# FFT filter and squared-ReLU FFN in one kernel: the FFT units of a batch spread over its whole period

## The chip, the cores and the metric

The kernel runs on one core of a Trainium2 chip. The metric is device time in microseconds. TensorE does the matmuls, VectorE (DVE) and ScalarE (ACT) empty PSUM and do elementwise work, GpSimd (POOL) and SyncE (SP) here mostly issue DMAs, each in its own order. The engines run side by side and wait for each other at semaphores.

## What is computed

```python
def _attn_ref(x, filt_r, filt_i):            # x: 8 x 3008 x 256
    X = np.fft.rfft(x, axis=1)
    F = (filt_r + 1j * filt_i)[None, :, :]
    Y = X * F
    return np.fft.irfft(Y, n=x.shape[1], axis=1).astype(np.float32)

def _moe_ref(x, w_in, w_out):                # x: 24064 x 256, w_in: 256 x 2048
    h = np.maximum(x @ w_in, 0.0)
    return (h * h @ w_out).astype(np.float32)
```

Each of the 8 batches is filtered along its 3008 positions; the result, as 24064 tokens, goes through two layers with a squared ReLU between them.

## The kernel before

**The FFT of a batch** is done by matmuls with constant matrices (3008 = 64 x 47), in four kinds of units:

- A (`unit_a`, L345): 16 a batch; one matmul of 512 columns into a psF tile, copied to `u` by ACT (even units, L362) or DVE (odd, L364); each four units are written to DRAM (`dU`) by SP. `load_x` (L186, POOL's queue) brings its input, two loads to a tile of four units.
- `read_u` (L429) brings a batch's `dU` back in another layout into the single buffer `ut`.
- B (`unit_b`, L436): 12 a batch; two matmuls of 256 columns into psF; DVE multiplies by the filter into `prod` (L450), and POOL issues two DMAs that add the halves of `prod` (L457).
- P (`unit_p`, L480): 12 a batch; two matmuls into psF, copied by ACT to `ze` (L489); each three units are written to DRAM (`dZ`, L492).
- `read_z` (L501) brings a quarter of `dZ` back into a tile `zt` by two DMAs (halves of the frequencies). The second half of every quarter needs the last P unit.
- Y (`unit_y`, L509): 16 a batch; four matmuls of 94 columns into psF, copied to `yt` by ACT (even) or DVE (odd, L532). Units 4c to 4c+3 read quarter c and give a quarter of the batch's tokens.

All psF tiles share two PSUM buffers, so a unit can only start when the unit two before it has been copied out.

**The FFN** goes over 47 groups of 512 tokens, each in 8 slots. In a slot, `ffn_g1` (L537) does four matmuls of 512 columns (more, where a group crosses a batch) and ACT's ReLU into `h`; `ffn_sq` (L559) squares on DVE, two slots at a time. The second layer of a group runs in the eight slots after, in one of two ways. The plain one (`ffn_g2`, L566) takes 64 matmuls of 256 columns. The other (`sums`, L627, and `products`, L655) takes seven products of half-size blocks instead of eight, 112 matmuls of 128 columns, for four sums on DVE and three adds into the output (L681, L687); the weights' own sums are made once (`make_t`, L611). `SEVEN` (L795) says which groups take it: from 9 on, save the last.

**The order** is written out by hand: every engine's instructions stand in program order. `fft_plan(b)` (L690) puts each unit of a batch at a slot relative to the batch's first one and at one of two places in it: 0, after the first layer's matmuls, or 1, after the second layer's. A batch's period is 48 slots (40 for batch 1). Batch b + 1's A units end where its `read_u` starts, five slots before its B. Batch 0 and most of batch 1's A units run in a prologue. The first tokens of batch b are needed by the first layer 48 slots after the batch's first (40 for batch 1).

```python
for s in range((NG + 1) * SLOTS):
    g, k = divmod(s, SLOTS)
    if g < NG:
        ffn_g1(g, k)
    run(work, s, 0)
...
    if (s - 1) // SLOTS - 1 in SEVEN:
        products((s - 1) // SLOTS - 1, (s - 1) % SLOTS)
    if g > 0 and g - 1 not in SEVEN:
        ffn_g2(g - 1, k)
    run(work, s, 1)
```

## Time and profile before

| | us |
|---|---|
| median of 3 runs | 782.75 (781.9 to 782.78) |
| the profiled execution | 782.47 |
| its span, first to last instruction | 780.7 |
| TensorE matmuls busy | 755.4 |
| DVE busy | 627.2 |
| ACT busy | 561.6 |
| POOL busy | 193.0 |

The granted TensorE clock is full throughout. Busy times of different engines overlap; a stretch's length is set by the engine that waits least in it. DVE's costs in the steady part, each from its group: a square of two slots 1218 ns (L564), a sum about 1217 ns (L639 to L648), an add into the output about 417 ns (L681, L687), a `prod` 1219 ns (L450), an A copy 683 ns (L364), a Y copy 546 ns (L532). ACT's: a ReLU 1024 ns (L557), a `ze` copy 588 ns (L489), an A copy 573 ns (L362), a Y copy 468 ns (L530).

### The profile page before, as it was taken

Reading aid. Unit: us, or ns where it says so; the run is one execution under the profiler, and the core shown is the slowest. Engines: PE = TensorE matmul, PEld = TensorE weight load, DVE = VectorE, ACT = ScalarE, POOL = GpSimd, SP = SyncE. Lnnn points to the kernel's source line nnn. Section 1 sums busy time; section 2 is a strip of 40 time slices with the busy share of each in tenths; the row PEclk is TensorE's granted clock in tenths of the full one; section 3 lists DMA queues with packets and bytes.
Section 4 is the critical chain, followed back from the end, with each engine's and each line's share of the span. In section 5 each row is a group of like instructions: output and inputs, shape, how many; then the busy total and the mean of one; then the engine's idle time right before and its main releaser. Section 6 shows DMA issues by size and latency. Waiting matters only on the chain. (4 is left out here: it accounts for less than half of the span.)

```text
span 780.7 us, 18857 instructions
## 1 busy us (share of the span) xinstructions
PE 755.4 (97%) x7878; PEld 552.5 (71%) x7878; DVE 627.2 (80%) x699; ACT 561.6 (72%) x785; POOL 193.0 (25%) x260
## 2 busy tenths in 40 slices
PE   8989999999999999999999999999999999999998
PEld 6746667667676676876778767777767767777776
DVE  6856644567778997899978999899988999987874
ACT  3976776767777677776777777776777767777774
POOL 3801730036100561005500065002840035100000
PEclk9999999999999999999999999999999999999999
DMA  9985974369534795167953578525875355521011
GB/s 365 375 253 160 149 161 116 89 158 175 136 80 119 169 171 145 57 180 130 171 116 96 173 127 149 154 76 158 149 145 126 89 151 128 128 78 55 29 55 55
DMA packets 104941, 109.20 MB, mean 140 GB/s; under 512 B 9640, under 2 KB 93096, under 8 KB 102936
## 3 DMA queue, kind: packets, MB, share of 16 engines
q1 hardware_dynamic: 85704, 87.38, 37.3%
q0 software_dynamic: 19008, 20.43, 19.5%
q8 instruction: 62, 1.02, 0.6%
q10 hardware_dynamic: 144, 0.18, 0.1%
q14 instruction: 23, 0.19, 0.1%
HBM read 58.12 MB, written 48.23 MB: 136 GB/s over the span
## 5 line engine op out<-in xcount | busy, mean ns | idle before, releaser
L557 ACT ACTIVATE h<-psH 128x1024 f16<-128x1024 f32 x376 | 384.6, 1024 | 172.2 <-PE psH L553 170.3
L553 PE MATMUL psH<-yt,sWin 128*128 128x512 f16 (+7 forms) x1728 | 386.9, 351 | 1.5 <-DVE yt L532 0.5
L564 DVE TENSOR_TENSOR h<-h 128x2048 f16<-128x2048 f16 (+1 forms) x192 | 229.6, 1196 | 64.8 <-ACT h L557 64.3
L457 POOL DMA_DIRECT2D prod<-prod x168 | 141.1, 997 | 463.7 <-DVE prod L450 458.4
L553 PEld LDWEIGHTS <-sWin 128*128 128x128 f16 x1728 | 153.4, 98 | 98.5 <-issue 3.4
L666 PEld LDWEIGHTS <-sum 128*128 128x128 f16 x2368 | 146.8, 98 | 27.2 <-issue 6.1
L666 PEld LDWEIGHTS <-h 128*128 128x128 f16 x1776 | 110.3, 98 | 22.5
L450 DVE TENSOR_TENSOR prod<-psB,sF 128x1024 f16<-128x1024 f32 x84 | 102.4, 1219 | 14.4 <-PE psB L442 14.4
L666 PE MATMUL psX<-sT,sum 128*128 128x128 f16 x1184 | 84.2, 219 | 0.0
L573 PE MATMUL psO<-sWout,h 128*128 128x256 f16 x640 | 81.8, 272 | 0.0
L573 PEld LDWEIGHTS <-h 128*128 128x128 f16 x640 | 62.0, 98 | 14.6 <-issue 0.2
L532 DVE CAST yt<-psY 128x376 f16<-128x376 f32 x62 | 33.8, 546 | 34.4 <-PE psY L523 34.4
L489 ACT CAST ze<-psP 128x512 f16<-128x512 f32 x84 | 49.4, 588 | 13.4 <-PE psP L487 8.9
L666 PE MATMUL psY<-sT,sum 128*128 128x128 f16 x592 | 57.2, 219 | 0.0
L666 PE MATMUL psY<-sWout,sum 128*128 128x128 f16 x592 | 44.9, 219 | 5.5 <-DVE bot L681 5.5
L364 DVE CAST u<-psA 96x512 f16<-96x512 f32 x50 | 34.1, 683 | 17.1 <-PE psA L358 14.9
L523 PE MATMUL psY<-sC,zt 112*128 112x94 f16 x512 | 42.4, 205 | 5.1 <-DMA zt<-dZ 4.9
L195 POOL DMA_DIRECT2D x<-in_x_dram x40 | 46.1, 1151 | 0.0
L642 DVE TENSOR_TENSOR sum<-sum,h 128x2048 f16<-128x2048 f16 x37 | 45.2, 1221 | 0.9
L666 PE MATMUL psY<-sWout,h 128*128 128x128 f16 x592 | 45.2, 219 | 0.0
L666 PE MATMUL psX<-sT,h 128*128 128x128 f16 x592 | 45.1, 219 | 0.0
L639 DVE TENSOR_TENSOR sum<-h 128x2048 f16<-128x2048 f16 x37 | 44.9, 1215 | 0.1
(88 smaller groups left out, 706.0 us busy)
## 6 DMA issues: line engine op xcount, KB each, us to landing
zt<-dZ SPq DMA_DIRECT2D x64, 192.0 KB
dU<-u SPq DMA_DIRECT2D x28, 384.0 KB
prod<-prod POOLq DMA_DIRECT2D x168, 64.0 KB, 3.6
dZ<-ze SPq DMA_DIRECT2D x28, 384.0 KB
x<-in_x_dram POOLq DMA_DIRECT2D x40, 192.0 KB, 5.3
ut<-dU SPq DMA_DIRECT2D x7, 1024.0 KB
xw<-in_x_dram SPq DMA_DIRECT2D x6, 1024.0 KB
ut<-dU SPq DMA_DIRECT2D x7, 512.0 KB
```

The costliest lines, as they stand in the source:

```text
L195: nc.gpsimd.dma_start(out=t, in_=v[:, m, :])
L450: nc.vector.tensor_mul(out=prod, in0=ps.rearrange("p (a d) -> p a d", d=D).unsqueeze(1).to_broadcast([128, 2, 2, D]), in1=sF[:, :, 2 * p:2 ...
L457: nc.gpsimd.dma_start(out=prod[64 * i:64 * i + 64, 0], in_=prod[64 - 64 * i:128 - 64 * i, 1], accum_op=mybir.AluOpType.add)
L489: nc.scalar.copy(out=zes[(b, c)][:, 2 * i6:2 * i6 + 2, :], in_=ps.rearrange("p (a d) -> p a d", d=D))
L523: nc.tensor.matmul(ps[:, 94 * jj:94 * jj + 94], zt[:, 4 * (g % 2) + jj, dt * 128:(dt + 1) * 128], sSY, start=True, stop=True)
L553: nc.tensor.matmul(ps[:, i, o:o + n], sWin[:, dt, jt * 128:(jt + 1) * 128], yts[b][:, dt, r:r + n], start=(dt == 0), stop=(dt == 1))
L557: nc.scalar.activation(out=h2[:, 2 * s:2 * s + 2, :], in_=ps, func=AF.Relu)
L564: nc.vector.tensor_mul(out=v, in0=v, in1=v)
L573: nc.tensor.matmul(pso[g][:, t % 2, :], h2s[g][:, jt, t * 128:(t + 1) * 128], sWout[:, jt, :], start=(jt == 0), stop=(jt == NJT - 1))
L639: nc.vector.tensor_add(out=t, in0=a21, in1=a22)
L642: nc.vector.tensor_sub(out=t, in0=f[5], in1=a11)
L666: nc.tensor.matmul(o[:, t, :], f[p][:, q, 128 * t:128 * t + 128], sg["w"][p][:, q, :], start=(m == 0 and p in (1, 2)), stop=(q == 7), skip ...
```

## The change

The plan now works in half slots, and units of one batch are spread over its period:

- A of batch b (3 and later) runs from slot -56 to -14.5 of the batch, one unit every 2.75 slots, a period ahead of its own B; all its copies go to ACT. A of batch 2 runs one unit every 1.25 slots from -30, with copies as before. `load_x` moves with A. Before the loads of batch 2, POOL copies one element of the current slot's `h` (`hold`), so that a load isn't issued before that slot.
- B runs from -5 to 38 instead of 18 to 36, and P 5 slots after its B, so from 0 to 43 instead of 22.5 to 40.5. Batch 1 keeps its B slots, with P 4.5 slots later. `prod` has five buffers instead of four.
- `read_z` of the four quarters stands at 43, 43.5, 48 and 54 instead of 41.5 (three) and 47.5; there are two `zt` tiles instead of three. The Y units stand at `YN`, from 45 to 72, instead of two a slot from 45 to 52.5. For batch 1 all of this is 7 slots earlier.
- `SEVEN` starts at group 6 instead of 9, and `make_t` does one of its four sums in each of four slots.

```diff
-    p_prod = ctx.enter_context(tc.tile_pool(name="p_prod", bufs=4))
+    p_prod = ctx.enter_context(tc.tile_pool(name="p_prod", bufs=5))
...
+    def hold(g, s):
+
+        nc.gpsimd.tensor_copy(out=tiny, in_=h2s[g][0:1, 2 * s, 0:1])
...
-        if a % 2 == 0:
+        if a % 2 == 0 or b > 2:
             nc.scalar.copy(out=o, in_=pv)
...
-    ztiles = [const.tile([112, 8, D], F16, name=f"zt_{c}") for c in range(3)]
+    ztiles = [const.tile([112, 8, D], F16, name=f"zt_{c}") for c in range(2)]
...
-        zt = ztiles[c % 3]
+        zt = ztiles[c % 2]
...
-        def put(r, place, f, *a):
-            plan.setdefault((r, place), []).append((f, a))
-
+        def put(r, f, *a):
+            r = int(2 * r)
+            plan.setdefault(divmod(r, 2), []).append((f, a))
+
+        d = 0
         if b == 1:
             for n in range(4, 16):
-                put(n if n < 8 else n + 2 if n < 12 else 2 * n - 7, n % 2, unit_y, 0, n)
+                put(YN[n] - (45, 45, 46, 46)[n // 4], unit_y, 0, n)
+            put(8, read_z, 0, 3)
             for k in range(4):
-                put((4, 5, 7, 7)[k], 1, cast_wout, k, nc.vector)
-        t0 = 2 if b == 1 else 5
-        for a in range(12 if b == 1 else 0, 16):
-            put(t0 + a // 2, a % 2, unit_a, b, a)
-        put(10 if b == 1 else 13, 1, read_u, b)
-        t0 = 14 if b == 1 else 18
+                put((4.5, 5.5, 7.5, 7.5)[k], cast_wout, k, nc.vector)
+            for a in range(12, 16):
+                put(2 + a / 2, unit_a, b, a)
+            put(10.5, read_u, b)
+            d = 7
+        elif b == 2:
+            for a in range(16):
+                if a % 2 == 0:
+                    put(-37 + 1.25 * a, hold, 0, 0)
+                    put(-37 + 1.25 * a, load_x, b, a // 2)
+                put(-30 + 1.25 * a, unit_a, b, a)
+            put(-8.5, read_u, b)
+        else:
+            for a in range(16):
+                if a % 2 == 0:
+                    put(-66 + 2.75 * a, load_x, b, a // 2)
+                put(-56 + 2.75 * a, unit_a, b, a)
+            put(-9, read_u, b)
         for p in range(12):
-            r = t0 + (15 if b == 1 else 18) * p // 11
-            put(r, 0, unit_b, b, p)
-            if b + 1 < B and 2 <= p < 10:
-                put(r, 0, load_x, b + 1, p - 2)
-            put(r + 4, 1, unit_p, b, p)
-        t0 = 34 if b == 1 else 41
+            r = 14 + 15 * p / 11 if b == 1 else -5 + 43 * p / 11
+            put(r, unit_b, b, p)
+            put(r + (4.5 if b == 1 else 5), unit_p, b, p)
         for c in range(4):
-            put(t0 if c < 3 else t0 + 6, 1, read_z, b, c)
+            put((43, 43.5, 48, 54)[c] - d, read_z, b, c)
         for n in range(16):
-            put((38 if b == 1 else 45) + n // 2, n % 2, unit_y, b, n)
+            put(YN[n] - d, unit_y, b, n)
         return plan
+
+    YN = (45, 45.5, 46, 46.5, 47.5, 49, 50.5, 52, 54, 56, 58, 60, 63, 66, 69, 72)
...
-    for c in range(2, 4):
-        read_z(0, c)
-
-    SEVEN = range(9, NG - 1)
+    read_z(0, 2)
+
+    SEVEN = range(6, NG - 1)
...
         for (r, place), w in fft_plan(b).items():
-            work.setdefault((first + r, place), []).extend(w)
+            for f, a in w:
+                if f is hold:
+                    a = divmod(first + r, SLOTS)
+                work.setdefault((first + r, place), []).append((f, a))
...
-        if s == SEVEN[0] * SLOTS:
-            make_t()
+        if SEVEN[0] * SLOTS <= s < SEVEN[0] * SLOTS + 4:
+            make_t(s % SLOTS)
```

More of the change, by code (lines that the diff above doesn't have):

```diff
@@ L257 @@
     sSP = const.tile([128, NC, 128], F16, name="sSP")
+    tiny = const.tile([1, 1], F16, name="tiny")
     sign = const.tile([128, 1], F32, name="sign")
@@ L609, with make_t @@
     sg = {}
-    def make_t():
-        t = p_t.tile([128, 4, 8, 128], F16, tag="t", name="sT")
+    def make_t(k):
         w = sWout.rearrange("p (q e) c -> p q e c", e=2)
@@ L616, in make_t @@
         b21, b22 = w[:, :, 1, 0:128], w[:, :, 1, 128:256]
-        nc.vector.tensor_sub(out=t[:, 0], in0=b12, in1=b11)
-        nc.vector.tensor_sub(out=t[:, 1], in0=b22, in1=t[:, 0])
-        nc.vector.tensor_sub(out=t[:, 2], in0=b22, in1=b12)
-        nc.vector.tensor_sub(out=t[:, 3], in0=b21, in1=t[:, 1])
+        if k == 0:
+            sg["t"] = p_t.tile([128, 4, 8, 128], F16, tag="t", name="sT")
+        t = sg["t"]
+        i0, i1 = ((b12, b11), (b22, t[:, 0]), (b22, b12), (b21, t[:, 1]))[k]
+        nc.vector.tensor_sub(out=t[:, k], in0=i0, in1=i1)
         sg["w"] = {1: b11, 2: b21, 3: b22, 4: t[:, 3], 5: t[:, 0], 6: t[:, 1], 7: t[:, 2]}
```

## The prediction

> **What bounds the kernel now.** I read the windows view first, with one stretch per batch: from the first matmul that a batch's Y units issue to the same matmul of the next batch. Columns: us, then busy time (and instructions) of PE, PEld, DVE, ACT, POOL, then granted clock, DMA share and GB/s.

> ```profile
> core 0: us, PE busy (x) PEld busy (x) DVE busy (x) ACT busy (x) POOL busy (x), PEclk, DMA share, GB/s
> ...
> 309.40:403.10 93.70, 91.17 (x1024) 68.11 (x1025) 84.13 (x94) 68.83 (x101) 24.07 (x32) 1.00 0.61 136
> 403.10:496.30 93.20, 91.17 (x1024) 68.56 (x1025) 84.10 (x94) 68.73 (x101) 24.07 (x32) 1.00 0.62 137
> ```

> A batch takes 93.7 us. Its matmuls need less. In the trace, matmuls of 512, 256 and 128 columns follow each other every 216, 109 and 56 ns. The 48 slots of a batch hold 192 first-layer matmuls of 512 columns (48 x 4 x 0.216 = 41.5 us), six groups of 112 products (37.5), and the FFT: A 16 x 0.216, B and P 24 x 0.109 each, Y 64 x 0.042 (11.4 in all). That makes 90.4 us, so TensorE is the bound and about 3.2 us per batch are gaps. DVE is at 84 of 93.7: close, so bursts can make TensorE wait. Which gaps they are is in the waits of PE:

> ```profile
> PE psY L666 <- DVE bot L681: 5.5, 5, 1.2
> PE psY L523 <- DMA zt<-dZ: 4.9, 7, 1.4
> ...
> PE psP L487 <- DMA prod<-prod: 2.6, 4, 0.7
> ...
> PE psP L487 <- DVE prod L450: 0.5, 2, 0.3
> ```

> The view counts idle time. Each gap costs some 0.16 us more, because a matmul is shown longer (379 ns) than the distance at which the next follows (216). Adding that, the DVE waits and the late prod transfers cost some 12 us over the whole run (with the small ones on psB and psX), and the waits for zt in batches 2 to 7 cost 4.5. The last are the end of a round trip through DRAM: the last product (unit P 11), its copy to ze, the write to dZ, the read into zt, the first Y unit. The timeline shows it for batch 3 (the row at 306.35 is SP's in a narrower window, where the reads that wait stand alone), and below it the start of batch 2's:

> ```profile
> 300.61 0.38 PE L487 MATMUL psP<-prod,sSP 128*128 128x256 f16 x2
> 301.06 0.58 ACT L489 CAST ze<-psP 128x512 f16<-128x512 f32 x1
> 302.38 0.40 SPq L604 DMA_DIRECT2D out_dram<-top  x1
> 302.87 0.45 SPq L492 DMA_DIRECT2D dZ<-ze  x1
> 306.35 2.19 SPq L505 DMA_DIRECT2D zt<-dZ  x5
> 309.44 0.33 PE L523 MATMUL psY<-sC,zt 112*128 112x94 f16 x4 [0.90 <-DMA zt<-dZ]
> ```

> ```profile
> 206.69 0.38 PE L487 MATMUL psP<-prod,sSP 128*128 128x256 f16 x2
> 206.89 1.02 ACT L557 ACTIVATE h<-psH 128x1024 f16<-128x1024 f32 x1 [0.23 <-PE psH L553]
> 207.81 0.58 ACT L489 CAST ze<-psP 128x512 f16<-128x512 f32 x1
> ```

> See three links in batch 3: from the product to the end of the copy 1.03 us; write issued 302.87, the read that needs it issued 306.35, so 3.48 us; then 3.09 us until the Y matmul runs. The write also stood behind an output store on SP's queue (301.64 to 302.87). Product to Y took 8.83 us here; in the seven batches it takes 8.0 to 8.8. In batch 2 the product follows straight on a first-layer matmul, so its copy waits for that ReLU and ends 1.70 us after the product.

> [...]

> **The change part by part.**

> *Seven products from group 6.* Groups 6, 7 and 8 go from 64 matmuls of 256 columns (64 x 0.1092 = 6.99 us) to 112 of 128 (6.25): -0.74 each, **-2.2 us**. DVE gets four sums (1.22 each) and three adds (0.42) more per group, 11.0 us in all with the squares; beside two to three prod and one or two Y copies that stays under the 15 us of a group. make_t in four slots (0.69 each) is hidden in DVE's slack.

> *Spreading.* DVE's load in the worst group before was 11.0 + 5 x 1.22 = 17 us, over the group's 15; after, prod come every 3.9 slots (2 or 3 a group) and for batches over 2 the eight A copies (0.68) are ACT's (0.57 each: ACT goes from 69 to 73 of 94). No group is then over 15. The bot waits and the late prod transfers go: **-12 us** (bounds -9 and -14; if DVE's spare were used up by something else they stay, +12 on my sum). x loads on POOL and read_u, 5 slots ahead of its B as before, keep their lead: 0.

> *The end of a batch.* P 11 moves from slot 40 (second half) to 43 (first half), read_z from 41 to 43, and Y 0 stays at 45. What was 4.5 slots is now 2. Between P 11 and Y 0 stand on PE: P 11, B 0 of the next batch and A 1 of the next but one (0.22 each) and two slots of 14 products and 4 first-layer matmuls (1.64 each, as 210.31 to 211.95 in the trace): 3.94 us. The round trip: copy end 1.70 (P now follows straight on first-layer matmuls, as in batch 2), write to read 3.2 (mean of seven, 3.0 to 3.5), read to Y 3.2 (3.0 to 3.6); SP has no store ahead in slot 43, which saves the 0.7 to 1.2 of before. 8.2 us; bounds 7.6 and 9.0. PE stands for 4.3 us before Y 0, with everything queued behind it. A 1 waits first: psF has two buffers, P 11 has its buffer until the copy ends, so 1.2 us of the 4.3 fall there. Six batches, with less PE work beside the last two (no A, no B): 4 x 4.3 + 4.5 + 4.7 = 26.4, less the 4.5 that were paid: **+21.9 us** (bounds 18 and 27).

> *Batch 1.* Same 4.5 slots, but read_z goes from slot 34.5 to 36, behind the store of slot 35. At 206.68 such a store held SP 2.2 us, until 3.1 us after the second layer's last matmuls began to drain. So the read is issued 3.6 us after slot 36 starts and lands near 6.7, while PE arrives at 4.6: **+2.1** (0 to 3). Y 3 of batch 1 now has B 1 of batch 2 ahead of it on DVE, and the first-layer matmuls behind it need it: **+0.7** (0 to 1.2).

> *psF.* A unit waits until the unit two before it is copied: some 1.6 us after an ACT unit in a slot's first half, 1.7 after a prod. The trace has that wait exactly: B 4 of batch 1 at 82.78, its prod until 84.42, P at 84.47 held for 0.44 us (0.27 idle and the 0.16).

> ```profile
> 82.78 0.38 PE L442 MATMUL psB<-ut,sSB 128*128 128x256 f16 x2
> 83.20 1.22 DVE L450 TENSOR_TENSOR prod<-psB,sF 128x1024 f16<-128x1024 f32 x1 [0.88 <-PE psB L442]
> 84.47 0.38 PE L487 MATMUL psP<-prod,sSP 128*128 128x256 f16 x2 [0.27 <-DVE prod L450]
> ```

> Laid over the new plan, slots 8 to 44 (A of batch 2 put among B, P and Y of batches 0 and 1) have 14 such pairs, 13 short by 0.3 to 0.6 us and one by 1.2: 6 us, against 1.6 before: **+4.5** (1 to 7). From batch 2 on, A 2 after Y 0 and B 3 after Y 8 are short by 0.3 and 0.5: **+3.5** over the run (0 to 6).

> *hold and the two z buffers.* Eight tiny POOL copies in slots 3 to 20 read h, so DVE's square waits for POOL there, behind up to two prod issues (1 us each). The groups there use the plain second layer and DVE has over 5 us spare a group: 0, at worst +1. A z buffer's last Y unit runs 1.5 slots or more before its next read, and the later quarters of Y end 8 slots or more before the first layer takes them: 0. Prod's fifth buffer and one memset (0.9 us) less: 0; gains are excluded, as nothing waits on them now.

> **Sum** on the profiled execution (span 780.7, its own time 782.47, so 1.8 around it): 780.7 - 2.2 - 12 + 21.9 + 2.1 + 0.7 + 4.5 + 3.5 = 799.2, hence 801.0. The median of the runs is 0.3 above that execution, less than the sum can tell.

> **Rivals.**
> *Faster.* The round trip is short in quiet queues. Then only the removals count: 780.7 - 2.2 - 12 - 4.5 + 3 = 765, time 767. For it: the reads before were issued six at once and stood behind stores. Against: the write alone took over 3.0 us in all seven batches, and batch 1, without a store ahead of it, still needed 3.1 for it. It decides at 8.2 - 18.5 / 6 = 5.1 us product to Y; below that the change wins.
> *The clock falls.* [...] Against: A 1 splits the wait in batches 2 to 5, leaving 3 us; only 6 and 7 have it whole.
> *DVE waits stay.* Prod after Y copies and squares still crowd the first slots of a group, and the 12 us are paid as well: 813. Against: nine us more slack a batch, and each stand of PE lets DVE catch up.

> **How the numbers follow.** Forecast 0.80, faster 0.07, no change (trip of about 5.1 us) 0.03, clock 0.06, DVE 0.04. The forecast's own bounds are 790 to 810; the range 787 to 812 leaves out most of the first rival, and half of the last two. 0.2% is 1.6 us, about what this kernel's runs can tell from no change. Faster 0.07, same 0.03, slower 0.90.

> **What would show it.** Right: PE waits for zt<-dZ of some 3 us in each of six batches; waits on bot and on prod transfers nearly gone; batch stretches of 95 to 96 us with PE busy the same; psA waiting on ze in slot 43. Wrong: P 11 to Y 0 under 5.5 us, or a batch stretch under 93, or PEclk under 1.00.

## The result, and the profile after

| | before | after |
|---|---|---|
| median, us | 782.33 | 830.8 (829.91 to 831.84) |
| span of the profiled execution, us | 780.7 | 829.6 |
| ratio | 1 | 1.062 (1.0602 to 1.0639) |

The change makes the kernel 6.2% slower, 48.5 us. The prediction said slower, but 801, and at most 812.

The windows view of the changed kernel, cut at the first Y matmul of batches 2, 3 and 4 (us, busy time of PE, PEld, DVE, ACT, POOL, clock, DMA share, GB/s), and the stretch from batch 2 to 3 before (the one from 3 to 4 stands in the prediction, at 309.40):

```profile
243.50:342.40 98.90, 92.77 (x1026) 68.34 (x1026) 80.13 (x86) 73.15 (x108) 24.08 (x32) 0.98 0.56 129
342.40:440.90 98.50, 92.87 (x1025) 68.92 (x1026) 80.22 (x86) 73.26 (x108) 24.09 (x32) 0.98 0.57 129
```

```profile
215.50:309.40 93.90, 91.15 (x1024) 67.17 (x1024) 84.12 (x94) 69.13 (x101) 24.07 (x32) 1.00 0.60 135
```

These two stretches take 98.9 and 98.5 us instead of 93.9 and 93.7. DVE's busy time fell from 84 to 80 us and ACT's rose from 69 to 73, as meant; both are far under the length of the stretch. The clock is no longer 1.00. In PE's waits the line for zt is now 32.4 us, where it was 4.9 before, and the waits for `bot` are gone:

```profile
PE psY L528 <- DMA zt<-dZ: 32.4, 10, 4.5
PE psA L363 <- ACT ze L494: 5.1, 7, 1.2
...
PE psB L447 <- ACT yt L535: 2.2, 6, 0.4
PE psA L363 <- DVE yt L537: 1.8, 2, 1.0
...
PE psP L492 <- DMA prod<-prod: 1.3, 2, 0.6
```

The timeline at the end of batch 3, the same place as shown of before. The SP row at 337.33 is from a narrower window, where the reads that waited for the write stand alone:

```profile
332.40 0.38 PE L492 MATMUL psP<-prod,sSP 128*128 128x256 f16 x2
332.62 0.38 PE L447 MATMUL psB<-ut,sSB 128*128 128x256 f16 x2
333.52 0.58 ACT L494 CAST ze<-psP 128x512 f16<-128x512 f32 x1
334.12 0.38 SPq L497 DMA_DIRECT2D dZ<-ze  x1
334.15 0.38 PE L363 MATMUL psA<-x,sC 94*96 94x512 f16 x1 [1.15 <-ACT ze L494]
336.03 1.01 POOL L199 DMA_DIRECT2D x<-in_x_dram  x1
337.33 1.28 SPq L510 DMA_DIRECT2D zt<-dZ  x3
342.36 0.33 PE L528 MATMUL psY<-sC,zt 112*128 112x94 f16 x4 [4.54 <-DMA zt<-dZ]
```

P 11 runs at 332.40, Y 0 at 342.36: 9.96 us, with 3.9 us of TensorE's own work between them. First A waits 1.15 us for the psF buffer that P 11's copy frees, then Y 0 waits 4.54 us for the read. Of the three links of the trip, the copy ends 1.70 us after the product and the read that needs the write goes out 3.21 us after it, both as forecast; the read until Y 0 takes 5.03 us instead of 3.2. Just after, TensorE runs at half speed. The windows view over that stretch:

```profile
342.36:342.94 0.58, 0.58 (x12) 0.58 (x13) 0.00 (x0) 0.22 (x1) 0.00 (x0) 1.00 0.10 21
342.94:346.36 3.42, 3.42 (x23) 2.17 (x21) 1.68 (x2) 1.21 (x3) 0.00 (x0) 0.50 0.02 5
346.36:350.00 3.64, 3.64 (x49) 2.95 (x48) 2.49 (x5) 2.88 (x5) 0.00 (x0) 1.00 0.00 0
```

The eighth column is the clock: 0.50 for 3.42 us, in which 23 matmuls run where the next 3.64 us hold 49. There are eight such stretches, one for batch 0 and one for each later batch, of 3.4 or 6.8 us, 41.0 us in all.

To see where the 48.9 us of span went, I took from each execution the distance from each matmul's start to the next one's, less the distance that its columns need at full clock, and put what is left down to the matmul that came late or to the half clock (us; under "prologue" everything up to 48 us but the warm-up; a row is good to somewhat under a microsecond):

| | before | after |
|---|---|---|
| needed by the columns | 744.6 | 742.4 |
| half clock, warm-up at the start | 1.5 | 2.5 |
| half clock, later | 0.2 | 17.7 |
| Y matmuls of batch 0 | 0 | 5.6 |
| Y matmuls of batch 1 | 0.4 | 3.3 |
| Y matmuls of batches 2 to 7 | 4.5 | 25.8 |
| A matmuls (psF) | 0.3 | 10.2 |
| second-layer products waiting for DVE | 6.9 | 0 |
| P matmuls | 5.0 | 3.0 |
| B matmuls | 0.8 | 3.2 |
| first layer, psO, prologue | 9.3 | 8.5 |

The seven products and DVE's relief are there, 2.2 and 6.9 us. They are outweighed fivefold by the waits of Y units (30 us more, nearly all of it for zt) and by the clock (18).

### The profile page after: what moved, and what is told of

Its sections match the earlier page's. It is cut to its first block, busy times and chain, and to the rows that moved or that the text cites. A ratio compares the mean times of both kernels' runs of the same rounds, so it can differ in the third digit from the quotient of the medians.

```text
span 829.6 us, 19171 instructions
## 1 busy us (share of the span) xinstructions
PE 773.1 (93%) x8022; PEld 562.8 (68%) x8022; DVE 622.7 (75%) x679; ACT 581.9 (70%) x831; POOL 194.0 (23%) x268
## 3 DMA queue, kind: packets, MB, share of 16 engines
q8 instruction: 63, 1.03, 0.5%
## 4 chain that ended last, share of the span: by engine, by line
PE 83%; DMA 8%; ACT 4%; DVE 3%; issue 1%; SPq 0%; POOL 0%; ACTq 0%; DVEq 0%; POOLq 0%
PE psH L558 36%; PE psX L671 17%; PE psY L671 12%; DMA zt<-dZ 5%; PE psO L578 4%; DMA dZ<-ze 3%; PE psY L528 3%; PE psA L363 2%; PE psB L447 2%; ACT h L562 2%; PE psP L492 2%; PE warm L277 1%; DVE prod L455 1%; ACT ze L494 1%; PE psf L296 1%
## 5 line engine op out<-in xcount | busy, mean ns | idle before, releaser
L558 PE MATMUL psH<-yt,sWin 128*128 128x512 f16 (+7 forms) x1728 | 392.7, 355 | 2.0 <-DVE yt L537 1.2
L671 PEld LDWEIGHTS <-sum 128*128 128x128 f16 x2560 | 161.8, 99 | 26.0 <-issue 3.6
L671 PEld LDWEIGHTS <-h 128*128 128x128 f16 x1920 | 120.0, 98 | 15.9
L671 PE MATMUL psX<-sT,sum 128*128 128x128 f16 x1280 | 95.0, 224 | 0.0
L528 PE MATMUL psY<-sC,zt 112*128 112x94 f16 x512 | 45.1, 214 | 33.9 <-DMA zt<-dZ 32.4
L528 PEld LDWEIGHTS <-zt 112*128 112x128 f16 x512 | 36.2, 103 | 57.1 <-issue 39.8
L671 PE MATMUL psY<-sT,sum 128*128 128x128 f16 x640 | 62.3, 220 | 0.0
L578 PE MATMUL psO<-sWout,h 128*128 128x256 f16 x448 | 59.2, 279 | 0.0
L367 ACT CAST u<-psA 96x512 f16<-96x512 f32 x90 | 52.3, 581 | 7.0 <-PE psA L363 5.5
L578 PEld LDWEIGHTS <-h 128*128 128x128 f16 x448 | 44.2, 100 | 14.6 <-issue 4.2
L535 ACT CAST yt<-psY 128x376 f16<-128x376 f32 x66 | 31.1, 472 | 27.6 <-PE psY L528 26.4
L647 DVE TENSOR_TENSOR sum<-sum,h 128x2048 f16<-128x2048 f16 x40 | 48.9, 1223 | 1.1
L653 DVE TENSOR_TENSOR sum<-h,sum 128x2048 f16<-128x2048 f16 x40 | 48.7, 1218 | 0.0
```

What stands on the lines that cost most here:

```text
L367: nc.scalar.copy(out=o, in_=pv)
L528: nc.tensor.matmul(ps[:, 94 * jj:94 * jj + 94], zt[:, 4 * (g % 2) + jj, dt * 128:(dt + 1) * 128], sSY, start=True, stop=True)
L558: nc.tensor.matmul(ps[:, i, o:o + n], sWin[:, dt, jt * 128:(jt + 1) * 128], yts[b][:, dt, r:r + n], start=(dt == 0), stop=(dt == 1))
L578: nc.tensor.matmul(pso[g][:, t % 2, :], h2s[g][:, jt, t * 128:(t + 1) * 128], sWout[:, jt, :], start=(jt == 0), stop=(jt == NJT - 1))
L647: nc.vector.tensor_sub(out=t, in0=f[5], in1=a11)
L653: nc.vector.tensor_sub(out=t, in0=a12, in1=f[6])
```

## The experiments

The theory: P 11 to Y 0 is a round trip through DRAM of about 8 us or more (8.1 to 8.8 before and 7.8 to 10.0 after, in batches 2 to 7), the change gives it two slots, and the stand that follows (a pause in which TensorE waits) also sets the clock to half. Rivals: spreading the units is the cost and Y only shows it; the clock falls for another reason; what lies beside the trip (x loads, read_u) makes it long.

**The round trip alone, in the kernel before (e7_late).**

```diff
-            put(r + 4, 1, unit_p, b, p)
+            if b == 1 or p < 11:
+                put(r + 4, 1, unit_p, b, p)
+            else:
+                put(43, 0, unit_p, b, p)
...
-            put(t0 if c < 3 else t0 + 6, 1, read_z, b, c)
+            put(*((t0, 1) if b == 1 and c < 3 else (43, 0) if c < 3 else (t0 + 6, 1)), read_z, b, c)
```

> The kernel before with one part of the change alone: P 11 and the reads into zt of batches 2 to 7 at slot 43 as in the change, all else as before. If the two-slot round trip and its clock are the cost, TensorE stands 8.0 - 3.5 = 4.5 us before Y 0 (0.75 now), and each stand is followed by 3.4 to 6.8 us at half clock: 782.5 + 6 x 3.8 + 6 x 2.5 = about 820. If the stands need the rest of the change (read_u and x loads near by), under 800.

Measured: 817.03, ratio 1.0432 (1.0398 to 1.0467). PE's waits in its trace, and the rows around Y 0 of batch 3:

```profile
PE psY L523 <- DMA zt<-dZ: 27.2, 7, 4.6
PE psY L666 <- DVE bot L681: 6.2, 5, 1.2
```

```profile
309.99 0.38 PE L487 MATMUL psP<-prod,sSP 128*128 128x256 f16 x2
318.08 0.47 PE L523 MATMUL psY<-sC,zt 112*128 112x94 f16 x4 [4.42 <-DMA zt<-dZ]
318.56 1.91 PE L666 MATMUL psX<-sT,sum 128*128 128x128 f16 x16
```

One unit and three reads moved in six batches bring 34 of the 48 us. The trip is 8.09 us here; the six range from 7.8 to 8.3. The waits for `bot` stay, since nothing else was changed. The 16 products after Y 0 take 1.91 us where they take 1.05 at full clock. The half clock costs some 13 us more than before in this trace (clock 0.977).

**The clock by itself (e9_latefill).** Matmuls on zeros fill the stand; their results are not used.

```diff
+        if n == 0 and b > 1:
+            fill = psF(f"fill_{b}")
+            for _ in range(16):
+                nc.tensor.matmul(fill, zero, sF[:, 0, 0:2, :], start=True, stop=True)
```

> The kernel of e7_late with 16 matmuls of 512 zero columns (3.5 us, results not used) ahead of Y 0 in batches 2 to 7, inside stands of 4.3 to 4.8 us. The stands stay as long; only the idle stretch shrinks to about 1 us. If the idle stretch sets off the halved clock, which costs 14 us in e7_late, the time falls to about 803 and the clock stays at 1.00 after the warm-up. If it has another cause, 817 as before.

Measured: 806.87, ratio 1.0297 (1.0279 to 1.0316), clock 1.00. The same rows of its trace:

```profile
312.37 3.62 PE L518 MATMUL fill<-sF,zero 128*128 128x512 f16 x16
316.98 0.33 PE L527 MATMUL psY<-sC,zt 112*128 112x94 f16 x4 [0.99 <-DMA zt<-dZ]
317.26 1.05 PE L670 MATMUL psX<-sT,sum 128*128 128x128 f16 x16
```

Ninety-six matmuls more, and 10.2 us less. The trip is as long (8.12 us), so only the idle stretch was taken away, and the products are back at 1.05 us. No half clock is left after the warm-up (some 13 us); that the time fell by only 10 is in the trace too: P's waits rose by 2 us, and stands and fill together take about 2 us more than the stands alone did. The same in the changed kernel with 12 matmuls (e2_fill):

> The changed kernel with 12 matmuls of 512 zero columns (2.6 us) added ahead of Y 0 in batches 1 to 7, inside the time that TensorE stands there; their results are not used. If the halved clock is a cost of its own, set off by the idle stretch, it stays at full speed after Y 0 and the time falls by about 14 to 817, although matmuls are added. If the clock falls for another reason, or costs nothing beside the wait, the time stays at 831 or rises.

Measured: 820.45, 1.048 (1.0453 to 1.0506). The half clock after the warm-up falls to some 7 us (clock 0.992, where the changed kernel has 0.975); waits for zt are still 15.0 us, the longest 2.6. So the clock is a cost of its own here, set off by the idle stretch; how much idle time went ahead of it is in the last section.

**More room for the trip in the changed kernel (e1_trip).**

```diff
-            r = 14 + 15 * p / 11 if b == 1 else -5 + 43 * p / 11
+            r = 14 + 15 * p / 11 if b == 1 else -5 + 38 * p / 11
```

> The changed kernel with the products over 38 slots instead of 43, so that P 11 stands at slot 38 and 7 slots lie before Y 0 in batches 2 to 7. If the two-slot round trip is the cause, the stands before Y 0 of batches 2 to 7 (25.8 us) and psA behind ze (3.6) go, and the clock halves no more in those batches (some 12 us of the 17): 831 - 41 = about 790. If spreading itself is the cost, and the Y unit is only where it shows, the waits turn up elsewhere and the time stays above 815.

Measured: 796.65, 1.017 (1.0146 to 1.0194); 34 us come back. The half clock is gone in batches 2 to 7 (clock 0.996, where the changed kernel has 0.975), the long stands too, and nothing shows up elsewhere in that size: spreading itself is not the cost. But in batches 2 to 6 TensorE still stands 1.2 to 2.0 us before Y 0, although seven slots lie between. SP's rows in batch 3 show why:

```profile
315.32 0.39 SPq L497 DMA_DIRECT2D dZ<-ze  x1
315.82 1.25 SPq L438 DMA_DIRECT2D ut<-dU  x2
...
319.47 4.40 SPq L510 DMA_DIRECT2D zt<-dZ  x4
```

The next batch's read_u (1.5 MB) goes out between the write and the reads; Y 0 runs at 327.17, 11.85 us after the write.

**read_u before the trip (e5_readu)**, on top of e1_trip.

```diff
-                    put(-66 + 2.75 * a, load_x, b, a // 2)
-                put(-56 + 2.75 * a, unit_a, b, a)
-            put(-9, read_u, b)
+                    put(-69.5 + 2.75 * a, load_x, b, a // 2)
+                put(-59.5 + 2.75 * a, unit_a, b, a)
+            put(-14.5, read_u, b)
```

> The kernel of e1_trip with A units and x loads of batches over 2 moved 3.5 slots earlier and read_u from slot -9 to -14.5, so that its 1.5 MB are read before the round trip. In e1_trip the read into zt took up to 7.1 us behind it, and stands of 1.2 to 2.0 us before Y 0 were left. If read_u's transfer is what lengthens the trip, these go (9.6 us in six batches): 796.7 - 9 = about 788. If the trip is long for another reason, the time stays at 796.

Measured: 800.76, 1.0212 (1.0177 to 1.0247). The stands before Y 0 of batches 2 to 7 are gone, as expected, and yet the time is 4 us longer than e1_trip's. The 1.5 MB now meet the prod transfers of B 11, and P 11 waits for them (5.1 us in all, a wait that e1_trip does not show):

```profile
PE psY L528 <- DMA zt<-dZ: 9.0, 4, 4.6
PE psP L492 <- DMA prod<-prod: 5.1, 6, 1.6
```

The 9.0 are batches 0 and 1, one wait of batch 1 alone 4.6. A and B units wait some 5 us more for psF buffers than in e1_trip, and the Y units of batches 0 and 1 with their half clock cost some 6 us more in this trace (clock 0.993, in e1_trip 0.996); why these two do was not traced. So read_u does lengthen the trip, but moving it moved the wait, and not only to P 11.

**x loads kept in their slots (e6_hold).**

```diff
+                    put(-66 + 2.75 * a, hold, 0, 0)
                     put(-66 + 2.75 * a, load_x, b, a // 2)
```

> The changed kernel with a hold before every x load of batches over 2 too, so that POOL issues none ahead of its slot. In batches 2 to 5 the read into zt took 4.1 to 5.0 us until Y 0, in 6 and 7, which have no x load, 3.3 and 3.0. If the load that runs ahead is the cause, it is 3.3 in all: 831 - 5 = about 825. If not (read_u's transfer then), the reads stay over 4 us and the time at 830 or above, for hold makes DVE's squares wait for POOL.

Measured: 828.27, 1.0562 (1.0531 to 1.0592). In the trace the read into zt until Y 0 took 3.2 to 3.4 us in batches 2 to 5 (338.48 to 341.86 in batch 3), against 4.1 to 5.0 in the changed kernel. The load at 336.03 in the timeline above, which POOL issues ahead of its slot, is what made the read longer. The time barely followed, since hold costs waits of its own: products for DVE 2.8 us instead of 0, A 14.5 instead of 10.2.

**Batch 0 as before (e4_early)**: its Y slots, its last two z reads in the prologue, three z tiles, and four prod buffers for room. The main lines of the edit:

```diff
-                put(YN[n] - (45, 45, 46, 46)[n // 4], unit_y, 0, n)
-            put(8, read_z, 0, 3)
+                put((n if n < 8 else n + 2 if n < 12 else 2 * n - 7) + n % 2 / 2, unit_y, 0, n)
```

> The changed kernel with the Y units of batch 0 at their slots of before, and three z tiles (and four prod buffers, for room) instead of two. If the moved Y units of batch 0 and their late z reads cost what the trace shows (63.9, 89.7 and the halved clock from 63), 831 - 4 - 3 = about 824. If these waits only move to the next unit, 829 to 831.

Measured: 825.73, 1.053 (1.0499 to 1.0561), 5 us less, near what was expected. Y 4 and Y 8 had been moved from slots 4 and 10 to 2.5 and 8, and in the changed kernel's trace they wait 1.20 and 2.24 us for their reads; here neither waits. Not all of this is sure to be the slots: in e1_trip's trace, with batch 0 as in the changed kernel, neither waits either, for there TensorE had already fallen back by a half-clock stretch at 49.9 us (clock 0.996 over that execution).

**The seven products from group 6, alone (e3_seven)** in the kernel before, and taken back in a good plan (e12_nine, below).

```diff
-    SEVEN = range(9, NG - 1)
+    SEVEN = range(6, NG - 1)
```

> The kernel before with only the seven products from group 6 instead of 9 (make_t in one slot as before). By the count of matmuls 782.3 - 2.2 = 780.1. The rival: DVE, with 4.9 us of sums and 1.3 of adds more in each of three groups in which batch 2's units run two a slot, holds TensorE back, and the time stays at 782 or above.

Measured: 783.6 against 782.69, 1.001 (0.9994 to 1.0027): nothing gained. The columns need 2.2 us less, but products waiting for DVE rise from 6.9 to 8.4 us and P's waits from 5.0 to 6.9: the rival.

**A version with both.** From these runs: batch 0 as in e4_early, batch 1's read_z at slot 34.5, read_u ahead of the trip, and units placed so that no unit's psF buffer is still being emptied.

> The kernel of e5_readu with batch 0's Y units and z tiles as in e4_early, batch 1's read_z at slot 34.5, and A of batch 2 and the later Y units moved by half slots so that few units follow a B or a copy too closely. What is left by the count: 782.5 - 2.2 (products) - 12 (DVE and prod waits) - 4.5 (waits before Y 0) + 5 (psF) = about 769. If DVE or psF hold TensorE back as before, 782 or above.

Measured: 787.14, 1.0046 (1.0029 to 1.0063). 10.4 us went to P units, behind DVE's Y copies (5.0) and prod transfers.

> The kernel of e8_best with products over 39 slots, P 6 slots after its B instead of 5, read_u one slot later, and the Y and A units moved again so that no P or Y follows a unit that DVE copies by under some 2.5 us. In e8_best 10.4 us went to P units that waited for DVE's Y copy (5.0) and for prod transfers (3.1). If these go and none come in their place, 787 - 9 = about 778; if each only moves to the next unit, 785 or above.

Measured: 781.92, 0.9991 (0.998 to 1.0001), no change. Those waits fell to 0.9 us, but one A unit a batch waited 1.25 us:

> The kernel of e10_best2 with the A units of batches over 2 one slot later (the first of each batch stays) and their x loads too, so that A 5 no longer shares half a slot with B 2 and Y 6. In e10_best2 A 5 waited 1.25 us for Y 6's buffer in each of five batches. If only this wait goes, 781.9 - 6.2 = about 776; if another takes its place, 780 or above.

Its core, against the changed kernel (`A2` lists batch 2's A slots, `YN` the new Y slots):

```diff
-            r = 14 + 15 * p / 11 if b == 1 else -5 + 43 * p / 11
+            r = 14 + 15 * p / 11 if b == 1 else -5 + 39 * p / 11
             put(r, unit_b, b, p)
-            put(r + (4.5 if b == 1 else 5), unit_p, b, p)
+            put(r + (4.5 if b == 1 else 6), unit_p, b, p)
...
-                put(-56 + 2.75 * a, unit_a, b, a)
-            put(-9, read_u, b)
+                put(-59 + 2.75 * a - (a == 0), unit_a, b, a)
+            put(-13.5, read_u, b)
...
+    YN = (45, 45.5, 46, 46.5, 48.5, 49, 50, 51.5, 54.5, 57, 60.5, 61.5, 62.5, 65.5, 69.5, 71)
```

Measured: 772.2 (771.93 to 772.61), ratio 0.9862 (0.9843 to 0.9882): 1.4% faster than the kernel before. Its windows view, over a batch, and its longest waits of PE:

```profile
400.00:492.00 92.00, 91.72 (x1029) 69.05 (x1028) 80.37 (x88) 73.61 (x110) 25.84 (x35) 1.00 0.61 139
```

```profile
PE warm L277 <- ACT zero L271: 2.7, 1, 2.7
PE psY L528 <- DVE u L369: 1.3, 1, 1.3
```

From Y 0 to Y 0 a batch takes 91.3 us, for 90.4 that the columns need. P 11 is at slot 40, five slots before Y 0, which runs 9.1 us after it without a wait in batches 2 to 5: TensorE has work for the whole trip.

> The kernel of e11_best3 with the seven products from group 9 again instead of 6. Alone on the kernel before (e3_seven) the earlier start brought nothing, 783.6 against 782.7. If that was DVE's crowding there, it brings its 2.2 us in the spread plan, and this run is at 772.2 + 2.2 = 774.4. If the count of matmuls doesn't decide even there, 772.2 or below.

Measured: 774.43 (773.92 to 775.94), 0.9899 (0.9881 to 0.9917). Where DVE has room, three groups more are worth the 2.2 us of their columns.

## Why the prediction was right or wrong

- *Seven products, -2.2*: right in the count (744.6 to 742.4), and shown by e12_nine against e11_best3. Not free of the rest: alone it gave nothing (e3_seven).
- *Spreading, -12*: products no longer wait for DVE (-6.9) and P's waits fall by 2.0; about 9 of 12, at the lower bound. The stands, in which DVE can catch up, are not needed for it: in e1_trip, without the long ones, no wait for `bot` is left either.
- *The end of a batch, +21.9*: right in place and nearly in size. Waits of Y units in batches 2 to 7 rose by 21.3, and A behind P 11 adds 3.6: 25, inside the bounds. The trip was taken at 8.2 us and took 7.8 to 10.0. The term that was off is the read until Y 0, put at 3.2 and 4.1 to 5.0 in batches 2 to 5; e6_hold shows that the x load beside it is the reason. The prediction had put the x loads at nothing.
- *Batch 1, +2.1 and +0.7*: +2.9, and nothing measurable for Y 3. The number is right by luck. The store did hold SP, until 135.72, but the read that Y 0 needs then waited 1.4 us more, until 138.09, for the write, which had been issued right after read_u's 1.5 MB and landed only some 6 us later (3.1 in batch 1 before); and the read took 4.6 us, with an x load issued beside it at 136.50:

```profile
129.19 0.89 SPq L438 DMA_DIRECT2D ut<-dU  x2
130.18 1.44 SPq L611 DMA_DIRECT2D out_dram<-ost  x3
131.73 0.39 SPq L497 DMA_DIRECT2D dZ<-ze  x1
```

```profile
138.09 1.26 SPq L510 DMA_DIRECT2D zt<-dZ  x3
```

- *psF, +4.5 and +3.5*: A waits 6.3 us more apart from those behind P 11, B 2.4: 8.7 for a forecast of 8. The sum is right partly by luck: A's part falls all before batch 2's first Y unit and is larger than forecast there (for all units together 4.5), and from then on only the wait of B 3 after Y 8 came (0.58 us in each of four batches), not that of A 2 after Y 0.
- *hold and the z buffers, 0*: wrong by 5.6 us, Y units of batch 0. Y 4 and Y 8 wait some 3.6 us for their reads, and Y 12 waits 1.7 us for a psF buffer (1.55 in the waits view, for DVE's prod). The text argued from when a z tile comes free; Y 4 and Y 8 were also moved 1.5 and two slots forward, ahead of their reads' arrival (batch 0 as before, e4_early, brought 5 us).
- *The step that failed is the rival of the clock*, given 0.06. It was put aside because A 1 splits the wait, "leaving 3 us". That 3 us is too short for the clock to fall was the author's estimate; the trace of before, whose waits for zt are 1.4 us at most, doesn't show it. The split happened (1.15 and 4.54 us in batch 3), but reads 0.9 to 1.8 us longer than forecast made up for it in batches 2 to 5. And 3 us was not too short: the clock was 0.50 after stands of 2.24 us (changed kernel, batch 0) and 2.25 us (e1_trip, batch 1), and in e6_hold, where these reads are as short as forecast, it was 0.50 in batch 2. The sum was also at odds with its own text: batches 6 and 7, with stands forecast at 4.5 and 4.7 us, have the wait whole there, and it put nothing down for the clock in them. Every batch paid: 17.7 us in eight stretches, 2.2 each. e9_latefill, at a clock of 1.00 with the stand filled, shows that this is the idle stretch's doing. Forecast 18.5 us, measured 48.9: the clock is 17.7 of the 30 us between them; batch 0 (5.6), the longer reads (3) and the smaller relief of DVE (3) are most of the rest.

So the sign and the mechanism of the wait were right, and the combination was missed: the clock's cost was treated as another outcome beside the stand when it follows from the stand. A sign that the text had named for being wrong came: a clock under 1.00. The two batch stretches shown are 98.9 and 98.5 us where it forecast 95 to 96.

## What to carry to other kernels

When work is spread evenly, look for the chain that doesn't spread: here last product, copy, write, read, first Y, 8.1 to 8.8 us from P 11 to Y 0 in batches 2 to 7 before and 7.8 to 10.0 after, and plan its distance first. Price a stand of TensorE as more than its length where the trace shows the clock fall after it (in the changed kernel eight times, for 3.4 or 6.8 us at 0.50, 2.2 us lost on average), and find what else is on the DMA engines in that stretch (the read until Y 0 took 4.1 to 5.0 us beside an x load, 3.2 to 3.4 without). Count an engine's relief only where that engine was the last to be waited for: DVE's brought 6.9 us here because products had waited for DVE that long.

## What the runs showed of the hardware

```profile
59.64:63.05 3.41, 1.09 (x4) 0.20 (x3) 3.41 (x5) 1.71 (x2) 0.00 (x0) 1.00 1.08 230
138.15:141.56 3.41, 1.40 (x8) 0.53 (x6) 1.23 (x1) 2.11 (x3) 0.00 (x0) 1.00 1.03 231
240.55:243.96 3.41, 0.43 (x9) 0.47 (x10) 0.00 (x0) 0.44 (x2) 0.00 (x0) 1.00 0.88 218
339.53:342.94 3.41, 0.58 (x12) 0.61 (x13) 0.00 (x0) 0.22 (x1) 0.00 (x0) 1.00 0.75 167
438.52:441.93 3.41, 1.04 (x20) 1.07 (x21) 0.00 (x0) 0.47 (x1) 0.00 (x0) 1.00 0.86 199
534.09:537.50 3.41, 1.21 (x11) 0.48 (x8) 0.62 (x1) 1.92 (x3) 1.44 (x3) 1.00 0.86 168
633.08:636.49 3.41, 0.00 (x0) 0.00 (x0) 0.02 (x1) 0.54 (x1) 0.00 (x0) 1.00 0.91 202
725.24:728.65 3.41, 0.16 (x1) 0.00 (x0) 0.11 (x1) 1.02 (x1) 0.00 (x0) 1.00 0.72 203
```

PE is busy for 1.40 us at most in these, so idle for 2.0 us or more. In the rest of that trace, taken in pieces of the same length and spacing, PE is idle for at most 1.8 us of a piece at full clock (435.11 to 438.52: 1.65 us busy), and the clock was 1.00 after each of them.

In the kernel before, taken in the same way, it is at most 1.4 us (46.89 to 50.30: 2.03 us busy), and the clock stays at 1.00.

Stands of like length went both ways. Batch 0's in the changed kernel, 2.24 us idle shortly after a wait of 0.96, and batch 1's in e1_trip, 2.25 us idle, were followed by a clock of 0.50. In e6_hold batch 3 stood idle 2.72 us, until 341.86, and kept its clock. The same view of e6_hold, in batch 2 and in batch 3:

```profile
241.19:244.60 3.41, 0.95 (x19) 0.98 (x20) 0.00 (x0) 1.22 (x2) 0.00 (x0) 1.00 0.71 174
244.60:248.01 3.41, 3.41 (x23) 2.03 (x21) 1.68 (x2) 1.27 (x3) 0.00 (x0) 0.50 0.02 5
336.76:340.18 3.42, 2.39 (x22) 1.30 (x20) 1.56 (x2) 2.28 (x3) 1.25 (x2) 1.00 0.98 231
340.18:343.59 3.41, 1.73 (x28) 1.57 (x29) 0.19 (x1) 0.81 (x3) 0.00 (x0) 1.00 0.67 126
343.59:347.00 3.41, 3.41 (x42) 2.50 (x41) 3.04 (x6) 2.64 (x5) 0.72 (x2) 1.00 0.00 0
```

In batch 2 one piece has 0.95 us of work, and the next one is at 0.50. Batch 3's stand lies across 340.18 (28 times 3.413 us after 244.60), so that its two pieces have 2.39 and 1.73 us of work, and the clock stays at 1.00.

With 16 matmuls on zeros in the stand the clock stayed at 1.00 (e9_latefill), and the 16 products after Y 0 took 1.05 us instead of the 1.91 of e7_late.

A read of 192 KB was 0.9 to 1.7 us longer with an x load (192 KB) issued shortly before it than without (4.1 to 5.0 us until Y 0 in the changed kernel, 3.2 to 3.4 in e6_hold, batches 2 to 5). In e5_readu, with read_u's 1.5 MB issued just ahead of them, P 11 of batch 4 could start only 8.6 us after the first of its two prod transfers was issued (408.17 to 416.77); the median of these from issue to landing is 2.9 us in that trace.
